# GeGLU feed-forward on one core: eight pairs' plain halves first, M1 held in hT

## The chip, the cores and the metric

One Trainium2 chip, one of its cores. The metric is the device time of one execution in microseconds; lower is better. The kernel before was timed three times.

## The reference

x is 2048 tokens by D = 1024; w_gate and w_up are 1024 by F = 3584, w_down is 3584 by 1024, all bf16.

```python
def reference(x, w_gate, w_up, w_down):
    return (_gelu(x @ w_gate) * (x @ w_up)) @ w_down
```

## The kernel before

The tokens are worked in two halves (h) of 1024, each in two blocks of 512. xT0 and xT1 hold the transposed blocks of a half (8 slices of 128 of D). For each half the hidden matrix hT (28 tiles of 128 of F, by 1024 tokens) is made from the gate and up weights, and then multiplied by w_down.

Both stages use a scheme with seven products in place of eight on a two by two split. In the first stage a *pair* is two tiles of F, top and bottom; D is split in two halves of four slices (KH = 4), the tokens in two blocks. For gate (j = 0) and up (j = 1) alike, M1 and M2 are plain products of the top tile with xT0 (bf16 weights); M5, M6, M7, M3 and M4 are products of sums: weight sums s1 to s4 and a22 (in s_mem, fp32) with token sums t1, t2, t3, b22 and t4 (in t_mem, fp32). Each product is four matmuls of 128 by 128 by 512 for each of gate and up, so that a pair on sums takes 56 matmuls; a pair in plain form takes 64. M1 is copied from its bank to a second one, since M1 alone goes on into M6, while M1 + M2 is a finished block.

`mm` (L415) issues a product's matmuls. `quads` (L406) works a group of two pairs: M1 for both, M2 for both, and then for each pair M6, M5, M7, M3, M4. Beside these, ScalarE copies M1 (L444), m5 (L472) and M6 (L478), takes gelu (L286) and casts a22 (L401). VectorE adds m5 into banks (`add_m5`, L434) and multiplies gate by up into hT (`mult`, L291). GpSimd makes s1 to s4 for the next pair (`s_sum`, L388) as soon as the product that read the slot is over. All instructions of an engine stand in the order in which they are written; the lists `thens` name what goes between the products (under the keys "m1", "start", "m6", "m5", "m7", "m3", "m4").

VectorE also prepares the down stage during the first half: 42 *stage steps* (L625) form sums of w_down rows, which `stage_load` (L611) brings and which are stored to a scratch tensor. In the first group 6 are issued, in later groups 9 (4 at "m1", 3 at "start", 2 at "m3"), and after them, in the list, four sums of hT (`s_down`, "s3", L670); the last group has just these four left, and two early ones.

The start of the first half is apart. Pair 0 (tiles 0 and 1) is in plain form for both token blocks (`part`, L323, and L267). Its xT0 comes half by TensorE transposes (L311), half by DMA transposes (L171), then xT1 by DMA transposes, then the rest of weight chunk 0. A *chunk* is the gate and up weights of four tiles, 2 MiB; two chunk places are in w_mem. Then pair 1 runs alone through `quads`, with its order M5, M6 and its first sums on VectorE for S3; one row of t4 is on GpSimd (L260). At most eight DMAs are in flight, by the eight semaphores that they take turns on. SP's and ScalarE's queues share the DMA engines.

Of the kernel before, what the change touches and what calls it, by code (L numbers as in the profile page):

```python
# [34 lines left out]
def kernel(  # L35
# [9 lines left out]
    P = 128  # L45
# [96 lines left out]

    xs0 = w_mem[:, 4 * CH : 4 * CH + TSB * D].rearrange("p (a b) -> p a b", b=D)
    chunks = {}

    def new_chunk(key):
        c0 = 2 * CH * (key[1] % 2)
        chunks[key] = tuple(
            w_mem[:, c0 + j * CH : c0 + (j + 1) * CH].rearrange(
                "p (a b) -> p a b", b=FG  # L150
            )
            for j in range(2)
        )
# [33 lines left out]
    load_x0(0, sp, 0, 2)  # L187
    load_x0(0, act, 2, TSB)
    load_w(first, 0, 0, 2, sp, 0, FA)
    load_x0(1, act)  # L190
    load_w(first, 1, 0, 2, sp, 0, FA)
    load_w(first, 0, 2, 5, act, 0, FA)
    load_w(first, 1, 2, 5, sp, 0, FA)
# [20 lines left out]
    load_xT(xT, 0, 0, KH, KH + 1)  # L214
    behind_transpose = last_on["sp"]
    load_xT(xT, 0, 0, KH + 1, KH + 2)
    for j in range(2):
        load_w(first, j, 5, KD, act, 0, FA)
        tc.add_manual_dep(
            last_on["act"].ins,  # L220
            behind_transpose.ins.name,
            SCHED_DEP,
            reason="engine order",
        )
    act(nc.scalar.preload_act_table(ACT.Gelu_apprx_tanh))
    load_xT(xT, 0, 0, KH + 2, KD)
    for k0, k1 in ((0, 2), (2, KH), (KH, KD)):
        load_xT(xT, 0, 1, k0, k1)
    for j in range(2):
        load_w(first, j, 0, KD, sp, FA, FG)  # L230
    new_chunk((0, 1))
    for j in range(2):
        load_w((0, 1), j, 0, KD)
# [31 lines left out]
    def mm_gu(ps, w_sb, fi, tb, kd):  # L265
        pe(
            nc.tensor.matmul(  # L267
                ps[:],
                lhsT=w_sb[:, kd, fi * P : (fi + 1) * P],
                rhs=xT[tb][:, kd, :],  # L270
                start=(kd == 0),
                stop=(kd == KD - 1),
            )
        )

# [23 lines left out]
    def unit_out(hT, bset, fi, tb):  # L299
        mult(hT, gelu(banks[bset[0]]), banks[bset[1]], fi, tb)  # L300

    def transpose_x0(q):

        parts = [(2 * q, 0, 4), (2 * q + 1, 0, 4)]
        if q == 0:
            parts = [(0, 0, 2), (0, 2, 4), (1, 0, 4)]
        for n, (kd, ts0, ts1) in enumerate(parts):
            tp = banks[(PB + QB)[(2 * q + n) % 4]][:].bitcast(BF16)
            for ts in range(ts0, ts1):
                pe(  # L310
                    nc.tensor.transpose(  # L311
                        tp[:, ts * P : (ts + 1) * P],
                        xs0[:, ts, kd * P : (kd + 1) * P],
                        ident[:],
                    )
                )
            cols = slice(ts0 * P, ts1 * P)
            if q == 0 or n == 0:
                dve(nc.vector.tensor_copy(out=xT[0][:, kd, cols], in_=tp[:, cols]))
            else:  # L320
                act(nc.scalar.copy(out=xT[0][:, kd, cols], in_=tp[:, cols]))

    def part(held, tb, k0, k1, us=(0, 1), js=(0, 1)):  # L323
        for kd in range(k0, k1):
            for j in js:
                for u in us:
                    mm_gu(banks[held[u][j]], chunks[first][j], u, tb, kd)

    def first_pair_units(hT):

        held = (VB, RB)
        transpose_x0(0)
        warm(RB[1], TB // 2)
        part(held, 0, 0, KPQ, js=(0,))
        transpose_x0(1)
        part(held, 0, 0, KPQ, js=(1,))
        part(held, 0, KPQ, KD)
        t_sum("t1", 0, KH // 2)
        t_sum("t1", KH // 2, KH)
        for u in range(2):  # L340
            unit_out(hT, held[u], u, 0)
        held = (QB, PB)
        part(held, 1, 0, KH)
        t_sum("t2")
        t_sum("b22")
        t_sum("t3", 0, KH // 2)
        part(held, 1, KH, KD, (0,))
        unit_out(hT, held[0], 0, 1)
        t_sum("t3", KH // 2, KH)
        part(held, 1, KH, KD, (1,))  # L350
        unit_out(hT, held[1], 1, 1)
        for j in range(2):
            s_sum(0, 1, j, "s3", True, False)
        for name in ("s1", "s2", "s4"):
            for j in range(2):
                s_sum(0, 1, j, name)
# [5 lines left out]
    def block(key, j, i, kh):  # L362
        fi = 2 * (key[2] % PPG) + i
        w_sb = chunks[(key[0], key[2] // PPG)][j]
        return w_sb[:, half(kh), fi * P : (fi + 1) * P]
# [40 lines left out]
    def quads(hT, h, members, nxt, thens, m5_first):  # L406

        last = nxt is None
        run = []
        for n, pair in enumerate(members):  # L410
            after = (h, members[n + 1]) if n + 1 < len(members) else nxt
            first_ = (PB, RB)[n] if len(members) > 1 else VB
            run.append((pair, after, thens[n], first_, (QB, VB)[n]))
# [27 lines left out]
        for pair, _, _, first_, q_ in run:  # L441
# [4 lines left out]
        for pair, _, _, first_, _ in run:  # L446
            for j in range(2):
                mm(first_[j], block((h, "p", pair), j, 0, 1), b21, False)
                if j == 0:
                    g = gelu(banks[first_[0]])  # L450
                else:
                    mult(hT, g, banks[first_[1]], 2 * pair, 0)

        V_, R_ = PB, RB
        for n, (pair, after, then, _, Q_) in enumerate(run):
            f0 = 2 * pair
            ends = after is None
            eager = "early" in then
# [10 lines left out]
            def do_m5(j):  # L469
                mm(V_[j], s(j, "s1"), tsum["t1"], True)  # L470
                m5[j] = m_pool.tile([P, TB], F32, name=f"m5_{j}")
                act(nc.scalar.copy(out=m5[j][:], in_=banks[V_[j]][:]))  # L472
                if not eager:
                    prep(j, "s1")
# [6 lines left out]
            if eager:  # L481
# [9 lines left out]
            for j in range(2):  # L491
                add_m5(Q_[j], Q_[j], m5[j])
                if not eager:
                    prep(j, "s2")
            done(n, "m5")
            for j in range(2):
# [4 lines left out]
                if j == 0 and eager:  # L501
                    pool_behind_dve()
                    for name in ("s1", "s2"):
                        for i in range(2):
                            prep(i, name)
                prep(j, "s3")
                if j == 0:
                    g = gelu(banks[V_[0]], ends)
                else:
                    mult(hT, g, banks[V_[1]], f0 + 1, 1)  # L510
# [9 lines left out]
            for j in range(2):  # L520
# [4 lines left out]
                else:  # L525
                    mult(hT, g, banks[R_[1]], f0 + 1, 0)
# [350 lines left out]
    for h in range(NH):  # L877
        hT = hT_pool.tile([P, KF, SH], BF16, name="hT")
        begin = 0
        if h == 0:  # L880
            first_pair_units(hT)
            xs = [(tb, kd) for tb in (1, 0) for kd in range(KD)]
            new_x(1)
            for i in range(3):
                stage_load(i)
# [7 lines left out]
            quads(  # L893
                hT,
                h,
                (1,),
                (h, PPG),
                (
                    {
                        "early": [],  # L900
                        "start": [lambda j=j: s_sum(0, 1, j, "a22") for j in range(2)]
                        + [lambda: t_sum("t4", 0, KH // 2)],
                        "m5": [lambda: t_sum("t4", KH - 1, KH, True)],
                        "v of gate": [lambda: t_sum("t4", KH // 2, KH - 1)],
                        "m4": [lambda: load_chunk((0, 2))],
                    },
                ),
                True,
            )
            begin = PPG  # L910
        s3_late = range(6, NS, 2)
        steps = [lambda k=k: stage_step(k) for k in range(NSTEP)]
        steps += [lambda i=i: s_down(hT, 0, "s3", i, i + 2) for i in s3_late]
        nstep, loads = len(steps), list(range(3, NS))

        def run_steps(n):
            for f in steps[:n]:
                f()
            del steps[:n]

# [8 lines left out]

        for lead in range(begin, NPAIR, PPG):  # L930
# [7 lines left out]
            if h == 0:  # L938
                few = lead == begin
                add(0, "m1", lambda n=3 if few else 4: run_steps(n))  # L940
                add(0, "start", lambda n=1 if few else 3: run_steps(n))
                for n in range(PPG):
                    add(n, "start", run_loads, run_x)
                    add(n, "m7", store_x, run_loads)
                    add(n, "m3", lambda: run_steps(1), run_loads)
            for n, pair in enumerate(members):
                if pair == NPAIR - 2:
                    add(
                        n,
                        "start",  # L950
# [117 lines left out]
```

## Time and profile before

| | us |
|---|---|
| runs (three) | 541.34, 540.13, 539.86 |
| median | 540.13 |
| profiled execution, its span | 537.4 |
| median less span | 2.7 |
| TensorE busy | 533.6 |
| VectorE, ScalarE, GpSimd busy | 367.6, 263.5, 252.2 |
| first stage, first half, by the chain of waits | 3.9 to 183.0 |
| down stage, first half | 183.0 to 270.9 |

The chain of waits lists what ended last at each moment, in order of time; here it is TensorE from 0.77 to 534.43 us. An engine's row in a timeline gives start, duration, line, operands and, in brackets, idle time before it with what ended it.

### The profile page before, as it was taken

What the parts mean: (1) busy time and instruction counts of PE and PEld (TensorE: products, weight loads), DVE (VectorE), ACT (ScalarE), POOL (GpSimd) and SP (SyncE); (2) the same over time, 40 slices, a digit from 0 to 9 for tenths busy, and PEclk for the clock granted to TensorE, in tenths of its full rate; (3) what the DMA queues carried; (4) which work ended last, traced back from release to release, by engine and by line L of the source; (5) the groups of instructions that cost most, each with busy time, mean ns of one, the idle gap of its engine ahead of it and who ended that gap; (6) DMA issues with size and microseconds to landing.
All of it is one profiled execution on the core that took longest, in us unless ns stands there. A gap on an engine that the chain in (4) does not pass through costs nothing.

```text
span 537.4 us, 7033 instructions
## 1 busy us (share of the span) xinstructions
PE 533.6 (99%) x2388; PEld 379.2 (71%) x2388; DVE 367.6 (68%) x476; ACT 263.5 (49%) x447; POOL 252.2 (47%) x213
## 2 busy tenths in 40 slices
PE   9999999999999999999999999999999999999997
PEld 4568686867677686777768676776768686866866
DVE  2985868787876998989555353444444669979961
ACT  2555555556465329117465554656555551452280
POOL 0698696969696200000056494958677670000000
PEclk9999999999999999999999999999999999999999
DMA  9965759697623887788950413314040329677846
GB/s 220 329 199 134 267 164 304 182 320 199 229 53 143 318 288 243 243 292 292 329 168 12 145 62 97 110 48 154 3 156 22 136 84 337 228 237 250 292 143 212
DMA packets 92547, 102.70 MB, mean 191 GB/s; under 512 B 18656, under 2 KB 67424, under 8 KB 92512
## 3 DMA queue, kind: packets, MB, share of 16 engines
q1 hardware_dynamic: 69568, 80.23, 45.7%
q10 hardware_dynamic: 22944, 22.02, 13.2%
q8 instruction: 19, 0.31, 0.3%
q14 instruction: 16, 0.13, 0.1%
HBM read 85.98 MB, written 12.58 MB: 183 GB/s over the span
## 4 chain that ended last, share of the span: by engine, by line
PE 99%; ACT 0%; issue 0%
PE bank L418 63%; PE bank L698 33%; PE bank L267 3%; PE bank L202 1%; PE bank L311 0%; ACT o_sb L754 0%
## 5 line engine op out<-in xcount | busy, mean ns | idle before, releaser
L418 PE MATMUL bank<-t_mem,s_mem 128*128 128x512 f32 x1056 | 244.6, 392 | 0.0
L418 PEld LDWEIGHTS bank<-t_mem,s_mem 128*128 128x128 f32 x1056 | 198.1, 188 | 42.7 <-issue 0.2
L388 POOL TENSOR_TENSOR s_mem<-w_mem 128x512 fp32r<-128x512 bf16 x102 | 124.0, 1236 | 185.5 <-DMA out_dram<-o_sb 96.9
L698 PE MATMUL bank<-t_mem,s_mem 128*128 128x512 f32 (+1 forms) x548 | 127.2, 391 | 0.0
L698 PEld LDWEIGHTS bank<-t_mem,s_mem 128*128 128x128 f32 x548 | 102.5, 188 | 22.0
L291 DVE TENSOR_TENSOR hT<-w_mem,bank 128x512 bf16<-128x512 f32 x106 | 72.5, 687 | 66.5 <-PE bank L418 44.5
L434 DVE TENSOR_TENSOR bank<-bank,m 128x512 f32<-128x512 f32 x108 | 70.0, 694 | 56.1 <-ACT m L472 54.3
L418 PE MATMUL bank<-xT,w_mem 128*128 128x512 bf16 x432 | 95.7, 379 | 0.0
L286 ACT ACTIVATE w_mem<-bank 128x512 f32<-128x512 f32 x106 | 63.0, 597 | 64.1 <-DVE bank L434 34.8
L418 PEld LDWEIGHTS <-w_mem 128*128 128x128 bf16 x432 | 41.2, 98 | 51.3 <-issue 3.4
L388 POOL TENSOR_TENSOR s_mem<-w_mem,s_mem 128x512 fp32r<-128x512 bf16 x52 | 68.4, 1335 | 2.9 <-PE bank L418 2.9
L600 DVE TENSOR_TENSOR t_mem<-w_mem 128x1024 fp32r<-128x1024 bf16 x56 | 65.9, 1225 | 0.9 <-PE bank L418 0.9
L388 POOL TENSOR_TENSOR s_mem<-s_mem,w_mem 128x512 fp32r<-128x512 f32 x52 | 61.3, 1200 | 0.0
L401 ACT CAST s_mem<-w_mem 128x512 fp32r<-128x512 bf16 x54 | 33.2, 616 | 31.3 <-PE bank L418 30.1
L478 ACT COPY bank<-bank 128x512 f32<-128x512 f32 x54 | 30.8, 570 | 26.6 <-PE bank L418 26.6
L670 DVE TENSOR_TENSOR s_mem<-hT 128x512 fp32r<-128x512 bf16 x52 | 36.7, 745 | 7.1 <-PE bank L698 7.1
L472 ACT COPY m<-bank 128x512 f32<-128x512 f32 x54 | 31.8, 589 | 18.4 <-PE bank L418 18.4
L698 PEld LDWEIGHTS <-hT 128*128 128x128 bf16 x224 | 21.3, 98 | 26.6 <-issue 2.1
L444 ACT COPY bank<-bank 128x512 f32<-128x512 f32 x54 | 30.7, 570 | 14.3 <-PE bank L418 13.5
L625 DVE TENSOR_TENSOR o_sb<-wd_sb,o_sb 128x512 fp32r<-128x512 bf16 x28 | 32.9, 1176 | 0.5
L763 ACT CAST o_sb<-bank 128x512 bf16<-128x512 f32 x27 | 14.8, 585 | 33.8 <-PE bank L698 33.8
L597 ACT CAST t_mem<-w_mem 128x1024 fp32r<-128x1024 bf16 x28 | 26.9, 1047 | 0.0
(46 smaller groups left out, 236.5 us busy)
## 6 DMA issues: line engine op xcount, KB each, us to landing
t_mem<-t_dram SPq DMA_DIRECT2D x56, 512.0 KB, 5.3
w_mem<-in_w_gate_dram ACTq DMA_DIRECT2D x10, 1024.0 KB, 5.4
w_mem<-in_w_up_dram ACTq DMA_DIRECT2D x10, 1024.0 KB, 8.3
wd_sb<-in_w_down_dram SPq DMA_DIRECT2D x28, 256.0 KB, 5.4
t_dram<-o_sb SPq DMA_DIRECT2D x28, 256.0 KB, 3.5
wd_sb<-in_w_down_dram SPq DMA_DIRECT2D x12, 512.0 KB, 7.6
w_mem<-in_w_down_dram SPq DMA_DIRECT2D x4, 1024.0 KB, 6.7
w_mem<-in_w_down_dram SPq DMA_DIRECT2D x8, 512.0 KB, 8.3
```

Source lines behind the costliest of these rows:

```text
L286: act(nc.scalar.activation(out=g_sb, in_=ps[:], func=ACT.Gelu_apprx_tanh))
L291: nc.vector.tensor_tensor(out=hT[:, fc, tb * TB : (tb + 1) * TB], in0=g_sb, in1=ps[:], op=ALU.mult,)
L388: pool(nc.gpsimd.tensor_tensor(out=t, in0=in0, in1=in1, op=op))
L401: act(nc.scalar.copy(out=t, in_=a(1, 1)))
L418: nc.tensor.matmul(banks[bank][:], lhsT=lhs[:, c, :], rhs=rhs[:, c, :], start=start and c == 0, stop=c == KH - 1, skip_group_check=True,)
L434: nc.vector.tensor_tensor(out=banks[dst][:], in0=banks[src][:], in1=m5[:], op=ALU.add)
L472: act(nc.scalar.copy(out=m5[j][:], in_=banks[V_[j]][:]))
L478: act(nc.scalar.copy(out=banks[R_[j]][:], in_=banks[Q_[j]][:]))
L600: dve(nc.vector.tensor_tensor(out=t, in0=in0, in1=in1, op=ALU.subtract))
L625: dve(nc.vector.tensor_tensor(out=t, in0=in0, in1=in1, op=ALU.subtract))
L670: dve(nc.vector.tensor_tensor(out=t, in0=in0, in1=in1, op=op))
L698: nc.tensor.matmul(banks[bank][:, c0:c1], lhsT=lhs(i, u), rhs=rhs(i)[:, c0:c1], start=start and i == 0, stop=stop and i == NS - 1, skip_gr ...
```

## The change

The first eight pairs of the first half are now made of tiles p and p + 8 (`LEAD`, `tiles_of`), so that tiles 0 to 7 are the top tiles and need, for M1 and M2, only chunks 0 and 1 and xT0. All M1 and M2 of the eight pairs come first, in `first_units`: for two tiles at a time the upper half of D (`top`), after which `hold` copies M1 from the bank to a place in hT that is not yet needed (`p_hold`), then the lower half (`rest`), gelu and mult. There are 128 plain matmuls there. Then `quads` runs with plain=False over the eight pairs: for each it copies M1 from hT back to a bank (`fetch`), and issues M5, M6, M7, M3, M4. Pair 0 is no longer in plain form: 56 matmuls in place of 64. Pairs 8 to 13 go as before, in groups of two.

Chunk 0 and chunk 3 now lie in hT's tiles 16 to 23 (`HELD`), chunks 1, 2, 4 and 5 in w_mem. In the queue of the start, chunk 0's lower half, chunk 1 and the half of chunk 2 with tiles 8 and 9 (the bottom tiles of pairs 0 and 1) stand ahead of the two transposes of xT1, the rest of chunk 2 behind them. The halves of chunk 3 go out on ScalarE's queue at the start of pairs 1 and 3, chunks 4 and 5 in pairs 4 and 7.

In pairs 0 to 7 both S3 sums of the next pair are on VectorE (`dve_too`); pair 0's own sums are all on GpSimd. t4 is wholly on VectorE. Of the stage steps one runs in pair 0, two in each of pairs 1 to 7, and nine in each of the three groups left; the four late s3 sums follow one by one at "m4" of pairs 8 to 11. The first loads of w_down rows into w_mem go out at "m7" of pair 11 in the first half, before at "start" of pair 12.

```diff
+    NL = 8
+    LEAD = tuple((p, p + NL) for p in range(NL))
+    HF = 2 * NL
+    HELD = ((0, 0), (0, 3))
+    def p_hold(pair, j):
+        if j == 1 and pair % 2 == 1:
+            return hT0[:, pair - 1 : pair + 1, TB:SH].bitcast(F32)
+        f = NL + pair if j == 0 else KF - 4 + pair // 2
...
+    load_xT(xT, 0, 0, KH, KD)
+    for f0 in (FA, 0):
+        for j in range(2):
+            load_w(first, j, KH, KD, sp, f0, f0 + FA)
+    new_chunk((0, 1))
+    for k0, k1 in ((0, KH), (KH, KD)):
+        for j in range(2):
+            load_w((0, 1), j, k0, k1)
+    new_chunk((0, 2))
     for j in range(2):
...
+        load_w((0, 2), j, 0, KD, sp, 0, FA)
+    for k0, k1 in ((0, KH), (KH, KD)):
         load_xT(xT, 0, 1, k0, k1)
     for j in range(2):
...
+        load_w((0, 2), j, 0, KD, sp, FA, FG)
...
+    def hold(held, tiles, j):
+        for u, t in enumerate(tiles):
+            act(nc.scalar.copy(out=p_hold(t, j), in_=bank2(held[u][j])))
+    def first_units(hT):
...
+        outs(*rest(1))
+        outs(*rest(0))
+        for j in range(2):
+            top(2, j, 0, KH)
+        for j in range(2):
+            top(3, j, 0, KH)
         t_sum("t1", 0, KH // 2)
         t_sum("t1", KH // 2, KH)
+        t_sum("t2")
+        outs(*rest(2))
+        t_sum("t3", 0, KH // 2)
+        t_sum("t3", KH // 2, KH)
         t_sum("b22")
+        outs(*rest(3))
         for j in range(2):
...
+            for name in ("s1", "s2", "s3"):
+                s_sum(0, 0, j, name)
+        for j in range(2):
+            s_sum(0, 0, j, "s4")
...
             def prep(j, name, after=after):
                 if after is not None:
-                    s_sum(after[0], after[1], j, name)
+                    dve_too = not plain and name == "s3"
+                    s_sum(after[0], after[1], j, name, dve_too, False)
...
+            if not plain and n + 1 < len(run):
+                fetch(n + 1)
             done(n, "m7")
...
+            thens[0]["start"] = [
+                lambda j=j: s_sum(0, 0, j, "a22") for j in range(2)
+            ] + [lambda: t_sum("t4", 0, KH // 2)]
+            thens[0]["m5"] = [lambda: t_sum("t4", KH // 2, KH - 1)]
+            thens[0]["v of gate"] = [lambda: t_sum("t4", KH - 1, KH)]
+            for n in range(1, len(LEAD)):
+                thens[n]["start"] = [lambda: run_steps(1), run_loads]
+                thens[n]["m3"] = [lambda: run_steps(1), run_loads]
+            thens[0]["m4"] = [lambda: new_x(1), lambda: run_steps(1), run_loads]
...
+            thens[1]["start"].append(lambda: load_half(0))
+            thens[3]["start"].append(lambda: load_half(FA))
+            thens[4]["start"].append(lambda: load_chunk((0, 4)))
+            thens[7]["m7"] = [lambda: load_chunk((0, 5))]
+            quads(hT, h, range(len(LEAD)), (h, begin), thens, True, False)
```

More of the change, by code (lines that the diff above doesn't have):

```diff
@@ L186 @@
     first = (0, 0)
[L187 to L193, printed above, removed]
+    for j, queue in enumerate((sp, act)):
+        ts = slice(j * TSB // 2, (j + 1) * TSB // 2)
+        load_x0(0, queue, ts.start, ts.stop)
+        load_w(first, j, 0, KPQ, queue, 0, FA)
+        load_x0(1, queue, ts.start, ts.stop)
+        load_w(first, j, 0, KPQ, queue, FA, FG)
+        load_w(first, j, KPQ, KH, queue)
     ident = const_pool.tile([P, P], BF16, name="ident")
@@ L403, with quads @@
     S_NAMES = ("s1", "s2", "s3", "s4", "a22")
-    def quads(hT, h, members, nxt, thens, m5_first):
-        last = nxt is None
+    def quads(hT, h, members, nxt, thens, m5_first, plain=True):
         run = []
@@ L411, in quads, with fetch @@
             after = (h, members[n + 1]) if n + 1 < len(members) else nxt
-            first_ = (PB, RB)[n] if len(members) > 1 else VB
-            run.append((pair, after, thens[n], first_, (QB, VB)[n]))
+            run.append((pair, after, thens[n], (PB, RB)[n % 2], (QB, VB)[n % 2]))
+        def fetch(n):
+            for j in range(2):
+                act(nc.scalar.copy(out=bank2(run[n][4][j]), in_=p_hold(n, j)))
         def mm(bank, lhs, rhs, start):
@@ L440, in quads @@
         b21 = xT[0][:, half(1), :]
-        for pair, _, _, first_, q_ in run:
+        for pair, _, _, first_, q_ in run if plain else ():
             for j in range(2):
@@ L445, in quads @@
         done(0, "m1")
-        for pair, _, _, first_, _ in run:
+        if not plain:
+            fetch(0)
+        for pair, _, _, first_, _ in run if plain else ():
             for j in range(2):
@@ L480, in quads @@
             done(n, "start")
-            if eager:
+            if not plain:
                 order = (do_m5, 0), (do_m5, 1), (do_m6, 0), (do_m6, 1)
@@ L891, in load_chunk @@
                         load_w(key, j, 0, KD, act)
[L893 to L910, printed above, removed]
         s3_late = range(6, NS, 2)
         steps = [lambda k=k: stage_step(k) for k in range(NSTEP)]
-        steps += [lambda i=i: s_down(hT, 0, "s3", i, i + 2) for i in s3_late]
+        lates = [lambda i=i: s_down(hT, 0, "s3", i, i + 2) for i in s3_late]
         nstep, loads = len(steps), list(range(3, NS))
@@ L938 @@
             if h == 0:
-                few = lead == begin
-                add(0, "m1", lambda n=3 if few else 4: run_steps(n))
-                add(0, "start", lambda n=1 if few else 3: run_steps(n))
+                add(0, "m1", lambda: run_steps(4))
+                add(0, "start", lambda: run_steps(3))
                 for n in range(PPG):
```

168 lines of the change are left out of this document (89 added, 79 removed).

## The prediction

> **What bounds the kernel now.** I read the chain of waits in order of time first, then the page's table of engines.
>
> ```profile
> PE 533.6 (99%) x2388; PEld 379.2 (71%) x2388; DVE 367.6 (68%) x476; ACT 263.5 (49%) x447; POOL 252.2 (47%) x213
> ```
> ```profile
> 6.87 12.95 PE bank L267 x60
> ...
> 270.92 175.56 PE bank L418 x784
> ```
> The chain is TensorE from end to end. 60 plain matmuls in 12.95 us are 0.216 us each. The 784 of the second half are 14 pairs of 12.54 us; 16 plain ones of a pair take 3.45 us, so its 40 on sums take 9.09 us, 0.227 each. Nothing waits: time changes by matmuls removed and by waits that appear. So the next question is how late VectorE and GpSimd run where the change puts work. The timeline of VectorE, then of GpSimd, at the start:
>
> ```profile
> 11.64 2.49 DVE L262 TENSOR_TENSOR t_mem<-xT,xT 128x1024 fp32r<-128x1024 bf16 x2 [4.54 <-DMA xT<-in_x_dram]
> 14.05 1.28 DVE L291 TENSOR_TENSOR hT<-w_mem,bank 128x512 bf16<-128x512 f32 x2
> 15.24 2.29 DVE L262 TENSOR_TENSOR t_mem<-xT,t_mem 128x2048 fp32r<-128x2048 bf16 x1
> 17.45 2.18 DVE L262 TENSOR_TENSOR t_mem<-xT 128x1024 fp32r<-128x1024 bf16 x1
> ...
> 20.14 1.58 DVE L262 TENSOR_TENSOR t_mem<-xT 128x1024 fp32r<-128x1024 bf16 x1
> ...
> 34.93 3.09 DVE L625 TENSOR_TENSOR o_sb<-wd_sb,o_sb 128x512 fp32r<-128x512 bf16 x2
> ```
> ```profile
> 17.32 1.22 POOL L388 TENSOR_TENSOR s_mem<-w_mem 128x512 fp32r<-128x512 bf16 x1 [16.01 <-DMA w_mem<-in_w_gate_dram]
> 19.06 1.58 POOL L388 TENSOR_TENSOR s_mem<-w_mem 128x512 fp32r<-128x512 bf16 x1 [0.52 <-DMA w_mem<-in_w_up_dram]
> ...
> 34.30 3.17 POOL L388 TENSOR_TENSOR s_mem<-w_mem 128x512 fp32r<-128x512 bf16 x2
> ```
> The reader is to see two things. The token sums t1 to t4 on VectorE started at 11.64, with xT1, and t1 and t2 were over at 17.53, when GpSimd's first sum had just begun. And the two engines slow each other when both read SBUF alone: a 1024-wide sum takes 1.25 us (2.49 for two) before GpSimd starts, 2.18 or 1.58 beside it; 512-wide ones come every 1.56 us on both engines at 34 us (3.09 less 1.53; 3.17 less 1.60), where the fastest rows alone are 0.68 and 1.17. A VectorE operation with a bank, such as mult, costs 0.60 in a row (1.28 less 0.68) and is not slowed.
>
> The windows give the rate of the transfers:
>
> ```profile
> 2.00:15.00 13.00, 13.00 (x65) 6.17 (x64) 4.67 (x8) 3.15 (x5) 0.00 (x0) 1.00 1.11 250
> 15.00:21.00 6.00, 6.00 (x30) 2.70 (x29) 6.00 (x5) 3.40 (x7) 3.16 (x3) 1.00 1.10 327
> 21.00:28.00 7.00, 7.00 (x33) 4.88 (x32) 7.00 (x8) 4.86 (x9) 7.00 (x5) 1.00 1.07 364
> ```
> The last column is GB/s; the queues are full (share 1.1) until 28 us.
>
> **The change, part by part.**
>
> *Matmuls.* The first pair in plain form is 64 at 0.216 = 13.8 us; as a pair on sums it is 12.54. Gain 1.27 us. All other matmuls stay, in another order.
>
> *When xT1 lands.* Before, xT1 ended 3 MiB into the queues. Now its first part (t1 needs it) ends 6.5 MiB into the queue: 1.05 MB of transposes, 3.67 MB in 512-byte rows (and the few 1 KB ones of chunk 0), 2.1 MB in 1 KB rows. From 2 to 15 us 3.25 MB moved, half of it transposes; with the plain half at 327 GB/s the transposes ran at 200. So 1.05/0.200 + 3.67/0.327 + 2.1/0.364 = 22.2 us, from 2.0: 24.2. A landing comes later than its share of the bytes: the second weight block that GpSimd waited for landed at 19.0 as byte 4.19 MB, when 4.56 MB had moved, 1.1 us late. I take 25.3; bounds 22.7 (all plain at 364, transposes at 250, 0.6 late) and 27.0 (2.8 late).
>
> *The sums of the second token block* are now a chain on VectorE from 25.3, and GpSimd works beside it, for its first sums wait for tile 8's weights, about 22. In VectorE's order: t1 in two parts 4.0 (between 1.58 and 2.18 each), t2 3.1 (2.29 and most of a GpSimd sum), two mult 1.2, t3 in two parts 4.2, two mult 1.2, half of t4 2.0, two add_m5 1.2, then t4's last two rows and an add 2.4, the new S3 of the next pair on VectorE 1.6 (before, this kind took 1.04 and 1.66 beside GpSimd), the second V add 0.7. Sum 21.6, end 46.9. With every sum at its lowest row beside GpSimd it is 17.9.
>
> *When TensorE needs it.* Plain products begin at 4.98 as before; two cold ones cost 0.55 more, 128 take 27.65, the transposes 0.45: M5 of pair 0 begins at 33.6. M4's second product begins 36 matmuls later, 8.2: 41.8, and it adds onto the bank that the V add reads. It waits 46.9 - 41.8 = 5.1 us, in several pieces (t3 for M7, the Q adds for M3, t4 for M4). Bounds: 2.5 to 6.8 by the landing, 1.4 with the short chain.
>
> By the Trainium skill, SBUF — State Buffer, section Who interferes with whom, a VectorE instruction with two SBUF inputs and a GpSimd instruction that reads SBUF exclude each other for the whole instruction. The trace agrees in kind, but two cost 1.56 us together, not the 1.73 of their sum alone; by the rule in full some eight of the chain's steps would each cost 0.17 more, 1.4 us in all.
>
> *The other transfers.* The first rest needs the lower half of chunk 0 after 32 matmuls, at 12.9; by the same rates its first half MiB is moved by 11.0 and landed by 12.1: taken 0, up to 1.0 if it is 2.8 late. The rest of chunk 2 and the rows for the stage steps now stand behind xT1 and end 9.5 MiB into the queue, about 34; their first readers come at 48. The down weights' first rows go out one pair earlier, 20 us ahead of use. All hidden.
>
> *Hold and fetch.* Each M1 was one ScalarE copy (0.57); now it is two, bank to hT (nearest row 0.589, bank to m) and back. 16 holds lie under 27 us of matmuls; one place is tight, two holds of 1.1 us under four matmuls of 0.86 ahead of the first rest: 0 to 0.3, taken 0. Fetches: ScalarE has 2 fetches, 4 copies, 3 gelu, 2 casts a pair, 6.5 us under 9.09.
>
> *The lead pairs 1 to 7* have 40 matmuls, 9.09 us. GpSimd: six sums at the page's mean of 1.26, 7.5. VectorE: seven bank operations 4.2, two S3 and two stage steps at the steps' mean (1.18, less the 0.08 by which the next one starts early), 4.4: 8.6. It fits, taken 0; with all four at 1.45 it is 10.0, over by 0.9 a pair. The two weight transfers on ScalarE's queue at the start of pairs 1 and 3 wait for GpSimd's last sum; behind them stand the m5 copies. That sum has M4 and half of M5, 2.7 us, and takes 1.6: nothing, unless GpSimd is over 1.1 late.
>
> *The last groups.* The pairs 8 to 13 take 9 stage steps a group now; before, the last group had only four light sums. In the group of pairs 10 and 11 before:
>
> ```profile
> 135.17 3.10 DVE L625 TENSOR_TENSOR o_sb<-wd_sb,o_sb 128x512 fp32r<-128x512 bf16 x2
> ...
> 140.50 1.41 DVE L625 TENSOR_TENSOR o_sb<-wd_sb,o_sb 128x512 fp32r<-128x512 bf16 x2
> 141.83 0.68 DVE L625 TENSOR_TENSOR o_sb<-wd_sb 128x512 fp32r<-128x512 bf16 x1
> 143.19 0.70 DVE L434 TENSOR_TENSOR bank<-bank,m 128x512 f32<-128x512 f32 x1 [0.68 <-ACT m L472]
> ```
> with nine steps the first Q add came 0.68 us after VectorE was free. The last group has the same nine and the two early s3 sums for the down stage, 0.6 and 1.5: 2.1 - 0.7 = 1.4 us that M3 waits. Bounds 0 to 2.2.
>
> Sum: -1.27 + 5.1 + 1.4 = +5.2 on a profiled span of 537.4 (the median of the runs is 2.7 above it): span 542.6, time 540.13 + 5.2 = **545.3**.
>
> **Rivals.**
>
> *The block lands in time (not slower).* If xT1's first part lands by 21 and the sums meet GpSimd only in their short form (17.9), the chain ends at 38.9, before 41.8; with the last group hidden too, only the gain is left: 540.13 - 1.27 = 538.9, and 540.3 with the last wait. For: the 1.58 row, and 364 GB/s late in the window. Against: six of the 6.5 MiB would need that rate, and transposes never showed it. It decides at a chain end of 41.8. 0.12, a third of it beyond 0.3%.
>
> *VectorE becomes the bound of the lead pairs.* At 1.45 for each S3 and step, seven pairs lose up to 0.9 each, 6.3: 551.6; at half of that 548.5. For: GpSimd is busy five sixths of such a pair. Against: the steps' mean is 1.18, and a VectorE operation that meets an idle GpSimd takes 0.68. It decides at a mean of 1.30. 0.10.
>
> *The clock falls.* The first seven matmuls ran 0.427 apart, and the fast spacing began 4.8 us after the first. A pause in pair 0 long enough to bring that back costs about 2.4 us: 547.7. Against: the wait comes in pieces of 1 to 2 us. 0.05. The Trainium skill (TensorE: Matmul & The Clock Gate, The HAM clock gate) puts the idle window at 3.4 us; no run here shows it.
>
> That the change does not do what it says I rule out: the engines' order has eight matmuls fewer, S3 on VectorE, and the transfers of tiles 8 and 9 ahead of xT1.
>
> **How the numbers follow.** Forecast 0.73, its own range 542.0 (landing at 22.7, half of the last wait) to 547.8 (landing at 27.0, last wait 2.2). With the rivals on both sides 8 in 10 is 541.3 to 549.0. A measurement of this kernel tells 0.3%, 1.6 us, from no change. Faster by more 0.04, within 0.08, slower by more 0.88.
>
> **What would show it.** Right: matmuls eight fewer; t1 starting near 25 on a DMA wait; VectorE without idle time from then to 47; TensorE waiting 4 to 6 us between 34 and 48, named to VectorE's t_mem and bank; a wait of about 1.4 at M3 of pair 12, near 175; 9.1 us a pair between. Wrong: t1 near 21, or no wait in pair 0; or lead pairs of 9.5 us and more; or a wait on ScalarE's queue at pair 1.

## The result: 548.2 us, 1.6% slower

The changed kernel took 548.2 us (median of four runs, 547.4 to 549.4) beside 540.0 for the kernel before on the same chip (539.5 to 541.3): a ratio of 1.0157, 95% interval 1.0135 to 1.0179. The forecast was slower, at 545.3 within 541.3 to 549.0. The measured time lies inside that range and just outside the forecast's own, 542.0 to 547.8. The profiled run has a span of 545.6 us, before 537.4. One run, the slowest of the twelve of e8 below (549.36 us at a granted clock of 0.990), counts as slow and is left out of the figures.

The engines' row of the page after:

```profile
PE 536.1 (98%) x2380; PEld 381.9 (70%) x2380; DVE 382.1 (70%) x495; ACT 274.2 (50%) x471; POOL 250.8 (46%) x206
```

Eight matmuls fewer, and TensorE's busy time is longer by 2.5 us while the span grew by 8.2. The chain of waits in order of time (start, length, what) says where. Before, it was TensorE from end to end. Now it is TensorE only from 48.34 us on, with one gap; ahead of that it runs through SP, whose issue of xT1's first transpose takes 6.26 us (SPq), and through VectorE:

```profile
18.62 6.26 SPq L196
...
34.47 1.27 DVE hT L301 x2
35.74 4.14 DVE t_mem L283 x2
...
47.68 0.62 DVE bank L489
48.34 123.04 PE bank L473 x540
...
175.83 1.64 DVE o_sb L677
177.47 0.62 DVE bank L489
178.23 12.96 PE bank L473 x56
191.19 87.89 PE bank L750 x392
279.08 175.56 PE bank L473 x784
454.64 87.95 PE bank L750 x396
```

The first stretch ends in M4's second product of pair 0 at 48.34, the second in M3 of pair 12 at 178.23. The lines left out between 24.88 and 34.47 are SP's next issues and a transfer of w_down rows; what held VectorE was xT1's landing, as its own timeline shows. From 191.19 on the stages are as long as before (the 784 matmuls took 175.56 then too): all of the loss lies in the first 191 us. VectorE's timeline in the first stretch (the last row is the second V add, which M4's second product waits for):

```profile
27.07 4.31 DVE L283 TENSOR_TENSOR t_mem<-xT,xT 128x1024 fp32r<-128x1024 bf16 x2 [6.10 <-DMA xT<-in_x_dram]
31.42 3.12 DVE L283 TENSOR_TENSOR t_mem<-xT,t_mem 128x2048 fp32r<-128x2048 bf16 x1
34.47 1.27 DVE L301 TENSOR_TENSOR hT<-w_mem,bank 128x512 bf16<-128x512 f32 x2
35.66 4.22 DVE L283 TENSOR_TENSOR t_mem<-xT 128x1024 fp32r<-128x1024 bf16 x2
39.80 1.27 DVE L301 TENSOR_TENSOR hT<-w_mem,bank 128x512 bf16<-128x512 f32 x2
41.00 2.09 DVE L283 TENSOR_TENSOR t_mem<-xT,t_mem 128x1024 fp32r<-128x1024 bf16 x1
...
46.02 1.66 DVE L439 TENSOR_TENSOR s_mem<-hT,w_mem 128x512 fp32r<-128x512 bf16 x1
47.60 0.69 DVE L489 TENSOR_TENSOR bank<-bank,m 128x512 f32<-128x512 f32 x1
```

The sums start with xT1's landing at 27.07 (11.64 before), VectorE is idle nowhere from then until 48.29, and t1's two parts take 4.31 where they took 2.49 before: GpSimd, which began at 23.59, is at work beside them, its sums at 2.0 to 2.2 us each:

```profile
28.28 2.02 POOL L441 TENSOR_TENSOR s_mem<-s_mem,hT 128x512 fp32r<-128x512 f32 x1
30.26 2.13 POOL L441 TENSOR_TENSOR s_mem<-hT,w_mem 128x512 fp32r<-128x512 bf16 x1
32.35 4.33 POOL L441 TENSOR_TENSOR s_mem<-hT,s_mem 128x512 fp32r<-128x512 bf16 x2
```

TensorE's part of it is a row of waits in pair 0, here from 30 to 49 us (total, number, longest):

```profile
PE bank L473 <- DVE hT L301: 1.3, 1, 1.3
PE bank L473 <- ACT bank L534: 1.2, 1, 1.2
PE bank L473 <- DVE bank L489: 0.8, 1, 0.8
PE bank L473 <- DVE t_mem L283: 0.5, 1, 0.5
```

The line with ScalarE is the same chain: the second copy of M6 goes into a bank that a mult operation had yet to read, and that mult stood behind t3 in VectorE's order:

```profile
41.19 0.57 ACT L534 COPY bank<-bank 128x512 f32<-128x512 f32 x1 [2.56 <-DVE hT L301]
```

In the second stretch, VectorE's timeline in the group of pairs 12 and 13, the four adds begin 1.65 us after TensorE could have used the first:

```profile
173.63 2.28 DVE L677 TENSOR_TENSOR o_sb<-wd_sb,o_sb 128x512 fp32r<-128x512 bf16 x2
175.83 1.64 DVE L677 TENSOR_TENSOR o_sb<-wd_sb 128x512 fp32r<-128x512 bf16 x1
177.40 2.48 DVE L489 TENSOR_TENSOR bank<-bank,m 128x512 f32<-128x512 f32 x4
```

### The profile page after: what moved, and what is told of

Its sections match the earlier page's. It is cut to its first block, busy times and chain, and to the rows that moved or that the text cites. A ratio compares the mean times of both kernels' runs of the same rounds, so it can differ in the third digit from the quotient of the medians.

```text
span 545.6 us, 7126 instructions
## 1 busy us (share of the span) xinstructions
PE 536.1 (98%) x2380; PEld 381.9 (70%) x2380; DVE 382.1 (70%) x495; ACT 274.2 (50%) x471; POOL 250.8 (46%) x206
## 4 chain that ended last, share of the span: by engine, by line
PE 89%; SPq 4%; DVE 3%; DMA 1%; issue 1%; ACTq 0%; ACT 0%; DVEq 0%
PE bank L473 57%; PE bank L750 32%; SPq L196 2%; SPq L185 2%; DVE t_mem L283 1%; DMA wd_sb<-in_w_down_dram 1%; DVE hT L301 1%; DMA hT<-in_w_up_dram 1%; DVE bank L489 1%; DVE o_sb L677 0%; SPq L663 0%; DVE s_mem L439 0%; DVE wd_sb L722 0%; ACTq L191 0%; ACT o_sb L806 0%
## 5 line engine op out<-in xcount | busy, mean ns | idle before, releaser
L473 PE MATMUL bank<-t_mem,s_mem 128*128 128x512 f32 x1096 | 256.8, 394 | 5.3 <-DVE bank L489 2.2
L473 PEld LDWEIGHTS bank<-t_mem,s_mem 128*128 128x128 f32 x1096 | 205.6, 189 | 53.5 <-POOL s_mem L441 3.4
L441 POOL TENSOR_TENSOR s_mem<-w_mem 128x512 fp32r<-128x512 bf16 x82 | 101.2, 1255 | 186.0 <-DMA out_dram<-o_sb 98.5
L750 PEld LDWEIGHTS bank<-t_mem,s_mem 128*128 128x128 f32 x548 | 102.5, 188 | 22.0
L296 ACT ACTIVATE w_mem<-bank 128x512 f32<-128x512 f32 x106 | 62.6, 597 | 62.9 <-DVE bank L489 41.5
L473 PE MATMUL bank<-xT,w_mem 128*128 128x512 bf16 x320 | 70.8, 379 | 0.0
L441 POOL TENSOR_TENSOR s_mem<-w_mem,s_mem 128x512 fp32r<-128x512 bf16 x46 | 59.7, 1320 | 5.9 <-PE bank L473 5.9
L473 PEld LDWEIGHTS <-w_mem 128*128 128x128 bf16 x320 | 30.5, 98 | 38.0 <-issue 2.6
L441 POOL TENSOR_TENSOR s_mem<-s_mem,w_mem 128x512 fp32r<-128x512 f32 x46 | 53.3, 1178 | 0.0
L534 ACT COPY bank<-bank 128x512 f32<-128x512 f32 x56 | 31.9, 570 | 27.4 <-PE bank L473 23.7
L454 ACT CAST s_mem<-w_mem 128x512 fp32r<-128x512 bf16 x48 | 29.5, 616 | 25.1 <-PE bank L473 22.4
L677 DVE TENSOR_TENSOR o_sb<-wd_sb,o_sb 128x512 fp32r<-128x512 bf16 x28 | 27.8, 991 | 0.3
L499 ACT COPY bank<-bank 128x512 f32<-128x512 f32 x40 | 22.8, 570 | 10.3 <-PE bank L473 10.3
```

Of the source, the lines that this page charges most:

```text
L296: act(nc.scalar.activation(out=g_sb, in_=ps[:], func=ACT.Gelu_apprx_tanh))
L441: pool(nc.gpsimd.tensor_tensor(out=t, in0=in0, in1=in1, op=op))
L454: act(nc.scalar.copy(out=t, in_=a(1, 1)))
L473: nc.tensor.matmul(banks[bank][:], lhsT=lhs[:, c, :], rhs=rhs[:, c, :], start=start and c == 0, stop=c == KH - 1, skip_group_check=True,)
L534: act(nc.scalar.copy(out=banks[R_[j]][:], in_=banks[Q_[j]][:]))
L677: dve(nc.vector.tensor_tensor(out=t, in0=in0, in1=in1, op=ALU.subtract))
```

## Experiments

In all of them the time is set against the kernel before on the same chip: its median was 539.1 beside e1 to e4, 539.4 beside e5 to e8 and 539.3 beside e9 to e11. On that scale the changed kernel is 8.2 above before (its first runs) and 9.1 (e5).

**e1: the second block earlier in the queue.** The edit moves the two transposes:

```diff
     for k0, k1 in ((0, KH), (KH, KD)):
+        if k0:
+            load_xT(xT, 0, 1, 0, KH)
+            load_xT(xT, 0, 1, KH, KD)
         for j in range(2):
             load_w((0, 1), j, k0, k1)
...
-    for k0, k1 in ((0, KH), (KH, KD)):
-        load_xT(xT, 0, 1, k0, k1)
```

> The second token block's two transposes stand ahead of chunk 1's lower half and of chunk 2 in the queue, nothing else is changed. Theory (the block's landing and the sums behind it on VectorE make pair 0 late): 2.1 MB less ahead of it at the 0.36 MB per us of the page is 5.8 us, so t1 starts near 21.3 and not 27.1. t1 and t2 are then over before GpSimd starts, t3 waits for the mult operations of the second rest (about 31), the chain ends near 44, M4's second product waits some 2.3 us and not 6.5: 544. First rival (GpSimd takes over): tile 8's weights now land near 27 and not 23.5, GpSimd's eight sums of pair 0 at 1.57 beside VectorE last until 40, TensorE waits for s_mem and, at pair 1, for ScalarE's queue behind the weight transfer: 546 to 547. Second rival (the landing is not what decides, the lock is): 548, the wait unchanged.

Measured: 548.15 us (546.05 to 550.48), 1.017 [1.013, 1.021] of before. t1 started at 21.61, 5.5 us earlier, and the second V add ended at 45.15, 3.1 earlier; yet the time did not fall. TensorE's and ScalarE's timelines show what took the gain:

```profile
45.20 6.43 PE L474 MATMUL bank<-t_mem,s_mem 128*128 128x512 f32 x20 [1.67 <-DVE bank L490]
51.94 6.23 PE L474 MATMUL bank<-t_mem,s_mem 128*128 128x512 f32 x26 [0.32 <-ACT bank L535]
```
```profile
48.28 0.37 ACTq L185 DMA_DIRECT2D hT<-in_w_gate_dram  x1
49.85 0.37 ACTq L185 DMA_DIRECT2D hT<-in_w_up_dram  x1
50.32 1.07 ACT L530 COPY m<-bank 128x512 f32<-128x512 f32 x2 [3.22 <-POOL s_mem L442]
```

20 matmuls took 6.43 us, where 20 at 0.227 are 4.5: seven of them stood 0.427 apart, behind pauses of up to 2.0 us. Then pair 1 waited 0.6 us for M5's copies, which stood on ScalarE's queue behind the weight transfer, and that behind GpSimd, whose first sum had moved from 23.59 to 28.75. So the first rival came true in GpSimd's lateness and in the wait at pair 1 (no wait for s_mem is named), and VectorE's chain was still 3.7 us late (45.2 against 41.5), for t3 waited for the mult operations of the second rest until 31.27. Between the runs the time goes with the granted clock: at 0.997 to 1.000 they took 546.05 and 546.38, at 0.993 and 0.994 they took 549.92 and 550.48. Only the run of 546.38 was traced.

**e2: GpSimd's sums of pair 0 ahead of the second block.**

```diff
     def block(key, j, i, kh):
         t = tiles_of(key[0], key[2])[i]
+        if key == (0, "p", 0) and i == 1:
+            t = 1
```

> GpSimd's eight sums of pair 0 and the cast of its a22 read tile 1 (chunk 0) where tile 8 belongs, so they wait for chunk 0 only and are over before the second token block lands; the products of pair 0 come out for the wrong tile. The queue is as in the changed kernel, t1 starts at 27.1. Theory (half of the long chain is the exclusion of GpSimd and VectorE): t1 2.5, t2 2.2, t3 2.5, half of t4 1.2 at their rows without GpSimd, six bank operations 0.6 each, so the chain that took 21.2 us ends about 5 us earlier, near 43; M4's second product waits 1 to 1.5 us: 543. Rival (only the landing counts, the sums are long whatever GpSimd does): 548, VectorE's sums as long as before.

Measured: 545.39 (544.88 to 546.04), 1.0118 [1.0103, 1.0134]: 6.3 above before, between the theory and the rival. xT1 as late as ever, and the sums short until pair 1's begin on GpSimd at 34.25:

```profile
26.91 2.36 DVE L283 TENSOR_TENSOR t_mem<-xT,xT 128x1024 fp32r<-128x1024 bf16 x2 [6.32 <-DMA xT<-in_x_dram]
29.30 2.29 DVE L283 TENSOR_TENSOR t_mem<-xT,t_mem 128x2048 fp32r<-128x2048 bf16 x1
...
32.70 2.35 DVE L283 TENSOR_TENSOR t_mem<-xT 128x1024 fp32r<-128x1024 bf16 x2
...
36.17 2.12 DVE L283 TENSOR_TENSOR t_mem<-xT,t_mem 128x1024 fp32r<-128x1024 bf16 x1
```

The same three sums took 2.36, 2.29 and 2.35 instead of 4.31, 3.12 and 4.22. The chain took 17.8 us (26.91 to 44.73) instead of 21.2. So GpSimd's eight sums cost the chain 3.4 us; 1.9 to 2.8 of them show in the time; six matmuls 0.427 apart behind the last wait took 1.2 back. What is left is the landing and the sums' own length: M4's second product began at 44.79, where 36 matmuls behind M5 would be 41.06.

**e3: two steps away from the start of pair 12.**

```diff
-                add(0, "start", lambda: run_steps(3))
+                few = lead == NPAIR - PPG
+                add(0, "start", lambda n=1 if few else 3: run_steps(n))
+                if few:
+                    add(0, "m7", lambda: run_steps(2))
```

> In the group of pairs 12 and 13 two of the three stage steps at the start of pair 12 are issued behind M7 of pair 12. Theory (the wait of 1.65 us at M3 of pair 12 is VectorE, busy with stage steps ahead of the Q adds): the wait goes, 546.5. Rival (the steps come late again behind M7, or the rows of the down stage that hang on them do): the wait turns up at M4 of pair 12 or at the start of the down stage, 548.

Measured: 547.04 (546.11 to 548.36), 1.0149 [1.0128, 1.017]: 8.0 above before. The wait at M3 of pair 12 is gone, so it was VectorE's work ahead of the Q adds; but the down stage now takes 88.7 us instead of 87.9, with a wait that was not there:

```profile
PE bank L750 <- DMA w_mem<-in_w_down_dram: 0.2, 1, 0.2
```

The rows it waits for were issued behind a mult operation that stood behind a late step in VectorE's order (in the chain: the step at 181.74, the mult from 182.79, SP's issues from 183.42 to 185.12, the rows' transfer from there to 195.41). Half of the gain came back as a late transfer.

**e4: S3 of the lead pairs on GpSimd.**

```diff
-                    dve_too = not plain and name == "s3"
+                    dve_too = False
```

> S3 of the lead pairs is computed on GpSimd again, eight sums a pair there, six bank operations, no S3 and two steps on VectorE. If GpSimd's sums keep the mean of 1.25 us, eight take 10.0 us in a pair of 9.09: seven pairs lose 0.9 each, 554. If, with VectorE's share smaller, they fall to 1.17 and two of them meet a step at 1.57, it is 10.2 as well. Rival (GpSimd has slack because VectorE excludes it less often, at 1.12 from start to start it is 9.0): 548, no change. A third outcome, faster than 548, would say that S3 on VectorE costs pair 0 its place in VectorE's chain (1.6 us ahead of the second V add) and gains nothing: 546.5.

Measured: 549.37 (548.92 to 550.66), 1.0196 [1.018, 1.0211]: 10.3 above before, 1 to 2 worse than with S3 on VectorE. None of the three came true as told: the pairs took 9.27 us (9.22 in the changed kernel), so GpSimd keeps up with eight sums, at 1.12 each where VectorE leaves it alone; but it is late enough to hold ScalarE's queue once, at pair 3:

```profile
69.40 0.38 ACTq L185 DMA_DIRECT2D hT<-in_w_gate_dram  x1
70.98 0.37 ACTq L185 DMA_DIRECT2D hT<-in_w_up_dram  x1
71.45 1.07 ACT L529 COPY m<-bank 128x512 f32<-128x512 f32 x2 [3.02 <-PE bank L473]
```

Both transfers waited for GpSimd's last sums of tiles whose memory they fill, M5's copies came behind them, and TensorE lost 2.0 us there. It is the wait that the prediction priced at nothing "unless GpSimd is over 1.1 late".

**e5: the changed kernel again.**

> The changed kernel once more, on the chip of the next three, for what its trace does from run to run. If the slow matmuls of pair 0 (0.427 us apart, six of them under the wait in the first trace) follow from the pauses, they turn up again, between 42 and 50; if they are an accident of that run they don't. xT1 between 26 and 28. 8.1 us slower than before.

Measured: 548.51 (547.45 to 550.26), 1.0175 [1.0158, 1.0193]. xT1 at 27.09; the second V add ended at 48.96; no matmul of pair 0 stood 0.427 apart in this trace, and the first stage ended at 191.72 (191.19): in the changed kernel itself the slow matmuls lie under VectorE's chain and cost nothing that shows.

**e6: the queue filled during SP's long issue.**

```diff
-    load_xT(xT, 0, 0, KH, KD)
     for f0 in (FA, 0):
         for j in range(2):
             load_w(first, j, KH, KD, sp, f0, f0 + FA)
+        if f0:
+            load_xT(xT, 0, 0, KH, KD)
```

> The transpose of the first block's lower half is issued behind the first two of the four lower weight blocks of chunk 0, not ahead of them. Theory A (SP takes 3.6 us to issue that transpose, and the queue runs thin meanwhile: 216 GB/s from 8 to 11 us): two more blocks, 0.5 MB, stand in the queue by then, which is 1.5 us of transfers, so everything behind lands 1 to 1.5 us earlier, t1 starts near 25.8, the wait of pair 0 is 5 and not 6.5: 6.8 us slower than before and not 8.1. Theory B (the landing follows the bytes ahead and nothing else): the bytes ahead of xT1 are the same, t1 starts at 27, 8.1 us slower than before.

Measured: 548.0 (546.24 to 550.39), 1.0163 [1.0141, 1.0186], no change. Chunk 1's first block landed 0.85 us earlier (16.38 against 17.23), and xT1 at 26.96 (26.98), as theory B had it; but the lead was lost on the way, at chunk 2's first block (23.45 against 23.52), and the bytes alone do not say why. SP began to issue xT1's first transpose 0.9 us earlier (17.71 against 18.62) and ended at the same time (24.80 against 24.88). So the long issue that the chain of waits names has no length of its own, and beginning it earlier did not bring the landing forward.

**e7: queue, VectorE's order and the weight transfers together.** On top of e1:

```diff
         t_sum("t2")
-        outs(*rest(2))
         t_sum("t3", 0, KH // 2)
         t_sum("t3", KH // 2, KH)
+        outs(*rest(2))
+        t_sum("t4", 0, KH // 2)
+        t_sum("t4", KH // 2, KH)
         t_sum("b22")
...
-            thens[1]["start"].append(lambda: load_half(0))
-            thens[3]["start"].append(lambda: load_half(FA))
-            thens[4]["start"].append(lambda: load_chunk((0, 4)))
+            thens[1]["m7"] = [lambda: load_half(0)]
+            thens[3]["m7"] = [lambda: load_half(FA)]
+            thens[4]["m7"] = [lambda: load_chunk((0, 4))]
```

> On top of the queue of e1 (t1 at 21.6 there), VectorE computes t3 right behind t2, ahead of the mult operations of the second rest, and the whole of t4 behind these, nothing of t4 in pair 0; and the weight transfers on ScalarE's queue are issued behind M7 of pairs 1, 3 and 4 and not at their start. Theory: t1, t2 and t3 are over near 28.7, when GpSimd begins; t4 takes 3 to 4 us beside GpSimd, over by 36; no step of the chain is left for pair 0 but the adds, and the Q and V adds come in time; GpSimd's eight sums end near 40. Pair 0 waits under 0.5 us, no slow matmuls, pair 1 does not wait for ScalarE; what is left is 0.08 to 0.13 at M7 of each lead pair and 1.65 at M3 of pair 12: -1.3 + 1.65 + 0.8 + 0.3, 1.5 us slower than before. Rival (GpSimd, which starts 5 us later than in the changed kernel, takes VectorE's place in pair 0): waits for s_mem of 2 to 3 us at M6 or M3 of pair 0, and slow matmuls behind them: 4 to 6 us slower than before.

Measured: 542.42 (541.09 to 543.49), 1.0056 [1.0041, 1.0071]: 3.0 above before, 6.1 less than the changed kernel beside it. TensorE's timeline has no wait in pairs 0 and 1 that it names; three of 0.1 to 0.3 us remain in the spacing:

```profile
33.37 32.82 PE L476 MATMUL bank<-t_mem,s_mem 128*128 128x512 f32 x138
```

No slow matmuls. The expected 1.5 left out 0.7 of such small waits; the profiled run itself is 541.72, 2.3 above before. What VectorE's order and the later weight transfers do each on their own was not separated.

**e8: the last two waits.** On top of e7:

```diff
-                order = (do_m5, 0), (do_m5, 1), (do_m6, 0), (do_m6, 1)
+                order = (do_m5, 0), (do_m6, 0), (do_m6, 1), (do_m5, 1)
...
-                add(0, "m1", lambda: run_steps(4))
-                add(0, "start", lambda: run_steps(3))
+                n1 = 4 + 1 * (lead == begin)
+                n2 = 3 + 0 * (lead == begin) - 1 * (lead == NPAIR - PPG)
+                add(0, "m1", lambda n=n1: run_steps(n))
+                add(0, "start", lambda n=n2: run_steps(n))
```

> e7, and two more edits. M6 of both halves stands between M5 of the first and of the second half in the lead pairs (R0's copy gets eight matmuls and not four before M7 reads it), and one stage step goes from the start of pair 12 to M1 of the group of pairs 8 and 9, where VectorE is busy 17.9 us of 25.1. Theory: lead pairs 9.09 us from start to start and not 9.2, M3 of pair 12 waits under 0.3, so only the matmuls removed are left: 1.3 us faster than before, 0.25%. Rival (the waits move: the step makes the Q adds of pair 8 or 10 late, or GpSimd's sums, whose S1 of the second half now comes 1.8 us later, hold M7): 0.5 to 1.5 slower than before.

Measured: 541.42 (539.46 to 547.20), 1.0051 [1.0027, 1.0075]: 2.0 above before, where 1.3 below was expected. The first half worked: from 60 to 100 us a matmul starts every 0.2267 us on the mean instead of 0.2308 in the changed kernel, 9.07 a pair instead of 9.22. What was late there shows in the changed kernel's waits of the weight loads from 57 to 113 us:

```profile
PEld bank L473 <- ACT bank L534: 1.4, 6, 0.2
```

Once a pair M7's first product waited for ScalarE's copy of M6 into R0, which had the four matmuls of M6's second half, 0.91 us, to lie under. The second half did not work: the step that was moved brought a new wait of 1.65 us at pair 8, and pair 12 kept 1.3. VectorE's timeline names a transfer:

```profile
116.90 1.48 DVE L680 TENSOR_TENSOR o_sb<-wd_sb 128x512 fp32r<-128x512 bf16 x1 [1.25 <-DMA t_dram<-o_sb]
...
170.15 1.48 DVE L680 TENSOR_TENSOR o_sb<-wd_sb 128x512 fp32r<-128x512 bf16 x1 [1.23 <-DMA t_dram<-o_sb]
```

With one more step early, the next one needs one of the four o_sb buffers whose store has not landed: in the chain that store takes 6.2 us at pair 8, behind a chunk of weights that lands at 115.05, and 8.0 at pair 12, where the down weights' rows were issued just ahead (the shortest took 2.0). The Q adds stand behind that step.

**e9: VectorE's order without the queue.** The edit of e7 on the changed kernel, without that of e1.

> VectorE's order of e7 (t1, t2, t3, then the mult operations, then all of t4, nothing of t4 in pair 0) and the later weight transfers on ScalarE's queue, with the queue of the changed kernel, so xT1 lands at 27. Theory (the landing has to come first, the order alone can't make up for it): t1 to t3 at 4.3, 3.1 and 4.2 beside GpSimd end at 38.7, the mult operations of the second rest come behind them and not at 34.5, the banks of the third rest are read late, and pair 0 waits 5 to 6.5 us in one piece near 39: 547 to 548.5, no gain over the changed kernel's 548.2. Rival (the order is what counts, e7's gain came from it): 543 to 544.

Measured: 548.47 (548.20 to 549.15), 1.0173 [1.0159, 1.0186], as the theory had it. The waits of pair 0 are one:

```profile
40.75 19.53 PE L475 MATMUL bank<-t_mem,s_mem 128*128 128x512 f32 x76 [5.83 <-DVE hT L301]
```

In this trace xT1 came 1.1 us later than in the changed kernel (t1 at 28.15, not 27.07), and seven slow matmuls behind the wait cost 1.4; without these the order alone might be worth 1 to 2 us (an estimate from this trace), where e7 gained 6. e1 alone and e9 alone gain nothing that the time shows; together they are e7. The landing has to be early and the sums have to be free to use it.

**e10 and e11: the steps to another place.** On top of e7, with the M5 and M6 order of e8:

```diff
-                add(0, "start", lambda: run_steps(3))
+                add(0, "start", lambda k=3 - (lead == NPAIR - PPG): run_steps(k))
...
-                    add(n, "m3", lambda: run_steps(1), run_loads)
+                    more = lead == begin and n == 0
+                    add(n, "m3", lambda k=1 + more: run_steps(k), run_loads)
```

(e11: no steps at the start of pair 12, one more at M3 of pairs 8, 9 and 10.)

> e7 with the M5, M6, M6, M5 order of e8 in the lead pairs, and one stage step moved from the start of pair 12 to M3 of pair 8, behind that pair's adds (in e8 it stood at M1 of that group, where a step waited for the store of an earlier one and pair 8 waited 1.65). Theory: e7's 3.0 above before, less 1.1 in the lead pairs (0.2267 a matmul as in e8, not 0.2308) and less the step of 1.6 at pair 12: 0.3 us above before, no wait at pair 8. Rival (the store of an earlier step stands behind the rows of the down weights again, and the step at pair 12 waits for its buffer as in e8): the wait of 1.3 to 1.5 at M3 of pair 12 stays, 1.9 above before.

> As e10, but all three steps leave the start of pair 12: one each to M3 of pairs 8, 9 and 10. Theory (pair 12's wait is the work that stands ahead of the Q adds, be it long steps or a step that waits for a store): no wait at pair 12 whatever the stores do, and the down stage 87.9 us as before: 0.3 above before. Rival (the steps at M3 are in the way there, with GpSimd at work beside them, or their stores collide): a new wait of 0.3 to 1.5 at pairs 9 to 11: 0.6 to 1.8 above before.

Measured: e10 541.51 (539.01 to 543.92), 1.0040 [1.0023, 1.0057]; e11 541.22 (539.37 to 543.90), 1.0036 [1.0021, 1.0051]. That is 2.2 and 1.9 above before, where 0.3 was expected. The wait of pair 12 is 0.2 in e10 and gone in e11, which has one of 0.6 at pair 10 instead, as its rival had it; none at pair 8. The profiled run of e10 took 539.01, the shortest of its twelve, 0.3 under before's median: the 1.27 us of matmuls, less a wait of 0.9 in pair 0 and the 0.2. What is late in pair 0 is now GpSimd, as TensorE's timelines of e10 and of e11 show:

```profile
35.75 24.57 PE L476 MATMUL bank<-t_mem,s_mem 128*128 128x512 f32 x107 [0.62 <-POOL s_mem L444]
```
```profile
37.63 22.54 PE L476 MATMUL bank<-t_mem,s_mem 128*128 128x512 f32 x98 [1.42 <-POOL s_mem L444]
```

Neither version beats before. Their runs spread over 4.5 to 4.9 us, where before's spread over 1.1. Of the 2.2 us between the two profiled spans, 537.2 and 539.4, the start has 1.1 (plain products over at 33.3 and 34.4, with waits for x and chunk 0), GpSimd 0.8 (its first sum comes 1.7 us later), the 0.6 at pair 10 against the 0.2 at pair 12 the rest. So in the two runs that can be compared most of the difference comes from when the early transfers land; that they do so in the others was not traced. To bring tile 8's weights forward as well, so that GpSimd starts earlier, was not tried.

## Why the prediction was right, and where its sum was off

**The mechanism held.** The second token block lands late, its sums on VectorE are long beside GpSimd, and M4's second product of pair 0 pays: e2 shortens the sums and e7 brings the block and the sums forward, and the time falls each time. e7 leaves 3.0 of the 9.1 us.

**The chain's length held:** 21.6 forecast, 21.2 measured (27.07 to 48.29). 4.31, 3.12 and 4.22 stand against 4.0, 3.1 and 4.2. Of the rule cited from the Trainium skill (SBUF — State Buffer, Who interferes with whom) e2 shows the kind (t1 in 2.36 us without GpSimd, 4.31 beside it), and the size went by the rows: with full exclusion the chain would have been 23.0.

**The landing was mis-sized:** 25.3 forecast, 27.0 measured, at the upper bound. The sum let 6.8 MB move by 24.2. By the windows of the changed kernel (the last column is GB/s), with 280 from 2 to 8 and 284 from 11 to 15, 6.3 had moved:

```profile
8.00:11.00 3.00, 2.61 (x13) 1.20 (x14) 0.00 (x0) 1.75 (x4) 0.00 (x0) 1.00 0.92 216
...
15.00:21.00 6.00, 6.00 (x30) 2.70 (x29) 2.57 (x4) 1.63 (x4) 0.00 (x0) 1.00 1.10 351
21.00:28.00 7.00, 7.00 (x34) 3.18 (x33) 0.93 (x1) 4.29 (x8) 4.33 (x4) 1.00 1.21 238
```

The missing 0.5 MB at 238 GB/s are 2 us, by this estimate. The thin stretch from 8 to 11 is not the cause, as e6 shows; chunk 1's first block landed at 17.2, where the forecast's rates and lag would have had it near 15.2, and from there to xT1 its 10 us held. Why the first 17 us ran slow is open, and in e6 a lead of 0.85 us at that block did not reach xT1. With M5 of pair 0 at 33.28 (33.6 forecast), the second product could start at 41.45 and started at 48.34: 6.9 us late and not 5.1 (the waits that are named come to 3.8 of them; the rest is short pauses and slow matmuls between).

**The lead pairs were not free:** taken 0, they cost 0.13 each, about 1.0 in eight. Neither GpSimd nor VectorE was it, the two that the step weighed, but ScalarE's copy, once M6 stands right ahead of M7 (e8). The order, M5 ahead of M6, was told with the change and was not priced.

**The last group:** 1.4 forecast, 1.65 measured, and by the cause that the step named (e3, e10).

**Little else appeared:** 0.4 us for chunk 0's upper rows near 8 us, and no wait for holds, for the first rest's weights or for ScalarE's queue at pairs 1 and 3. The last one was near: e1 and e4 brought it on by making GpSimd later. With these, -1.27 + 6.9 + 1.0 + 1.65 + 0.15 (a copy at pair 10) - 0.3 (M5's earlier start) is +8.1; the span grew by 8.2.

**The rivals.** The block does not land in time, and VectorE does not bound the lead pairs. The falling clock is real but not the cause here: e5 has none of it in its trace and is no faster. What the prediction held against it, that the wait comes in pieces of 1 to 2 us, does not hold (see the last section). That the sum came within 2.9 us owes little to luck: what it missed, the landing and the lead pairs above all, has the same sign and does not cancel.

## What to carry to other kernels

Loading something ahead of a late operand is free only if the operand's whole chain is counted, landing, sums and what stands between them on their engine: moved alone, the transfer (e1) or the sums (e9) brought nothing that the medians show, and both together gave back 6 of 9 us. When an engine's queue is cleared, ask what next one step behind it is late: here ScalarE's queue behind GpSimd, a store behind a bulk load, a copy with four matmuls to hide under. And a gain of 1.3 us in matmuls isn't worth a start that depends on the order in which 7 MB of transfers land.

## What the hardware showed that was not expected

The clock falls in pauses that are short. In e1 seven matmuls stood 0.427 us apart from 46.6 on, where the others stand 0.227 apart, though no pause was longer than 2.0 us. Where a trace has such a fall, the granted clock is halved for 3.41 us (in e9 for 6.83), and the full clock ahead of it lasted 10, 11 or 12 times 3.41. So I count in windows of that length. A row gives the window, its length, TensorE's busy time and matmuls, then the other engines; the third number from the end is the granted clock. In e1:

```profile
42.93:46.34 3.41, 1.73 (x7) 1.15 (x7) 3.41 (x5) 2.24 (x5) 3.41 (x3) 1.00 0.01 2
46.34:49.75 3.41, 3.41 (x10) 2.63 (x9) 3.38 (x5) 0.62 (x1) 3.41 (x3) 0.50 0.05 11
```

And in e5, where the clock stays up:

```profile
38.12:41.53 3.41, 1.90 (x7) 0.78 (x5) 3.41 (x4) 0.83 (x2) 3.41 (x3) 1.00 0.00 0
```

Windows with 1.46 to 1.66 us of work (e2, e3, e6, the changed kernel) were followed by the half clock, windows with 1.79 to 2.06 (e3, e4, e5, e11) by the full one; at 1.73, e1's fell and one in e8 did not. So in these traces the clock falls when TensorE was busy in less than about half of a window, and where the windows lie against the pauses differs from run to run. The Trainium skill (TensorE: Matmul & The Clock Gate, The HAM clock gate) speaks of an idle window of about 3.4 us that runs freely. The traces agree in its length; idle it need not be. In e9 a single pause of 6.2 us brought seven slow matmuls.

GpSimd beside an idle VectorE takes 1.12 us from one 512-wide sum to the next (24.82, 25.94 and 27.05 in the changed kernel); in e4 it did eight in a pair of 9.27 us. The mean of the profile's page of before, 1.26, has VectorE's share in it, and is no price for a pair in which that share changes.
